# A recurrent attention with a gated feed-forward layer: the ordering list is searched anew with the weight additions one by one, and the last bank goes in two halves

## The chip, the cores and the metric

The kernel runs on one core of one Trainium2 chip. The metric is the device time of one execution in microseconds (us); lower is better. Five engines work side by side: TensorE (PE, with its weight load PEld), VectorE (DVE), ScalarE (ACT), GpSimd (POOL) and SyncE (SP), which issues most of the DMAs.

## The reference

The first part is a recurrence over 768 tokens for 4 batches and 8 heads of 48 dimensions, the second a feed-forward layer on the 3072 tokens:

```python
for t in range(S):
    cur = np.einsum('bhd,bhe->bhde', u[None] * kt, vt)
    y[:, :, t] = np.einsum('bhd,bhde->bhe', rt, state + cur)
    state = w[None, :, :, None] * state + np.einsum('bhd,bhe->bhde', kt, vt)
...
h = x @ w_in                       # 3072 x 384 by 384 x 2048
g = h * np.clip(h + 3.0, 0.0, 6.0) / 6.0
return g @ w_out                   # 3072 x 2048 by 2048 x 384
```

## The kernel before

**Attention.** The recurrence is done in 24 half steps i = 0 to 23 of 64 tokens for two batches (`attention`). `prepare` scales k and r by powers of w (tiles ks and RP), makes the bonus term (rt, bt, X); a *visit* is one block of small TensorE products: `keep` adds k v to the state in the bank U, `scores` of the next step fills the bank SC, `outputs` makes the result from the state St and from X. `choose` puts the masked scores into X (the row named COPY_PREDICATED or "mask"). After a visit VectorE makes the state product St (L710) from U, and ScalarE copies St back into U (L702); the next visit reads both. Visits and state products are numbered from zero by i. From step 6 on a visit holds the scores of the next step too.

**Feed-forward.** The weights come as 64-bit words (raw) and are turned into a high and a low part, w (`weights`: z, cv on VectorE and ScalarE, "CAST w" and "w<-z,w"). Tokens go in 6 groups of 512. In the groups 0 and 1 a unit is one of 16 blocks f of 128 hidden rows: nine products of 512 columns into h (L361), relu and gate (t on ScalarE and VectorE, g on ScalarE and VectorE), nine products into the banks o (L368). The groups 2 to 5 go in two passes of two groups with a scheme that saves products: inputs, weights and intermediate banks are added and subtracted, so that fewer products (`product`, L890) are needed. The sums of the weights for two blocks f and f+1 are made by `sums` into the tile zf: one large addition of w's high and low part (L861) and four small ones on quarters of zf (L864); ScalarE or VectorE rounds zf to S, and VectorE or GpSimd takes the rest (L852). There are 8 such pairs in each of two passes. `second` makes the output products of the one group in the banks o, `beside` those of the other group in the banks h0 (hA), SC (hC) and Y (hD), one bank after the other; VectorE adds a bank divided by 6 to the tile part (L929), and `store` writes it.

**What sets the order.** Every piece is recorded as an operation with its cost on each engine that may do it (`S.add`). `Schedule.order` then makes one list for all engines at build time: among the operations that can start, the one with the highest priority goes first. The priority is the length of what follows plus a number from the table SHIFT; the table HOME fixes the engine of single operations. Operations with `port=True` exclude each other on VectorE and GpSimd in this plan. Where TensorE would be idle, the plan may put dummy products (`warm`, L1071). Only the order of the instructions on each engine goes to the chip; there semaphores set the times.

The additions of `sums` were one operation, on GpSimd alone:

```python
S.add({"pool": 3.0}, ws, ["zf"], emit, 0.0, True, deps=[fresh])
```

The last bank of the program is that of `outside(2, ...)`: `beside` puts two times three products into Y, VectorE adds, SP stores 128 rows of 512 columns.

Of the kernel before, what the change touches and what calls it, by code (L numbers as in the profile page):

```python
# [17 lines left out]
ALU = mybir.AluOpType  # L18
# [188 lines left out]
    "pool", 1191: "dve", 1193: "dve", 1205: "pool", 1209: "act", 1216: "act", 1220: "act", 1258: "dve", 1287: "dve",  # L207
    1289: "dve", 1292: "act", 1294: "pool", 1310: "dve", 1321: "dve", 1333: "dve", 1337: "dve", 1349: "dve", 1376:
    "dve", 1388: "dve", 1399: "dve", 1413: "dve", 1416: "dve", 1450: "pool", 1452: "dve", 1454: "dve", 1489: "dve",
    1493: "act", 1494: "pool", 1516: "dve", 1530: "dve"  # L210
}


# [1020 lines left out]
```

## Time and profile before

| | |
|---|---|
| median of three runs | 479.52 us (478.64 to 482.89) |
| the profiled execution: its time | 478.21 us |
| the profiled execution: its span | 476.1 us |
| TensorE busy | 458.7 us, 96% of the span |
| VectorE busy | 363.1 us, 76% |
| ScalarE busy | 220.3 us, 46% |
| GpSimd busy | 155.6 us, 33% |

The span is what the trace covers; 2.1 us of the execution's time lie around it. Busy shares are means over stages that are unlike each other: the attention steps lie in the first 345 us, the products of the last 120 us stand alone. A product of TensorE overlaps the next, so that its own duration is longer than its pace.

### The profile page before, as it was taken

To read this page: it belongs to the slowest core of one execution; us is meant where nothing else is said; L and a number is where in the kernel's file an instruction comes from. 1 tells how busy PE (TensorE), PEld (TensorE's weight loads), DVE (VectorE), ACT (ScalarE), POOL (GpSimd) and SP (SyncE) were. 2 spreads that over 40 slices of the span, in tenths; PEclk is the share of its full clock that TensorE was granted. 3 is DMA by queue.
4 is the path that set the end of the run, shared out by engine and by line. 5 is a ranking of instruction groups with operands and counts; after the bars stand their busy time and mean duration, and the time that the engine had idled before them with its cause. 6 is when DMAs were issued, how large, how long until landed. Compare 5 with 4: busy or idle time off the path is not lost.

```text
span 476.1 us, 11775 instructions
## 1 busy us (share of the span) xinstructions
PE 458.7 (96%) x4914; PEld 377.6 (79%) x4914; DVE 363.1 (76%) x553; ACT 220.3 (46%) x386; POOL 155.6 (33%) x156
## 2 busy tenths in 40 slices
PE   8889899999998999999999999999999999999994
PEld 6778788888887888777778878888688888888883
DVE  6989999989999983999597686464976456664553
ACT  5465757653434533554443344354653434343441
POOL 2173111124366630364452345235133213321100
PEclk9989999999999999999999999999999999999998
DMA  7977654483434612341220220000120000000003
GB/s 213 271 234 217 215 156 132 141 246 123 125 118 151 194 45 78 91 136 43 77 89 22 79 90 20 8 1 7 47 88 3 1 1 0 1 0 0 1 0 138
DMA packets 27038, 42.91 MB, mean 90 GB/s; under 512 B 4034, under 2 KB 12867, under 8 KB 26979
## 3 DMA queue, kind: packets, MB, share of 16 engines
q1 hardware_dynamic: 26882, 42.00, 29.0%
q8 instruction: 40, 0.66, 0.6%
q14 instruction: 20, 0.16, 0.1%
q10 hardware_dynamic: 96, 0.10, 0.1%
HBM read 35.98 MB, written 4.72 MB: 85 GB/s over the span
## 4 chain that ended last, share of the span: by engine, by line
PE 73%; DVE 16%; issue 3%; DMA 3%; ACT 2%; SPq 1%; ACTq 0%; DVEq 0%
PE o L368 21%; PE h L890 17%; PE h L361 10%; PE Y L368 5%; PE SC L890 4%; PE h L368 4%; PE SC L368 4%; PE Y L890 2%; PE SC L561 2%; DVE ks L458 2%; DMA rT<-rT 2%; PE h L561 1%; PE Y L561 1%; DVE RP L458 1%; DVE g L458 1%
## 5 line engine op out<-in xcount | busy, mean ns | idle before, releaser
L368 PE MATMUL o<-g,w 128*128 128x512 f32 (+1 forms) x594 | 143.0, 385 | 0.7 <-issue 0.7
L368 PEld LDWEIGHTS o<-g,w 128*128 128x128 f32 x594 | 108.8, 188 | 23.1 <-issue 0.9
L361 PE MATMUL h<-XR,w 128*128 128x512 f32 (+1 forms) x306 | 72.2, 380 | 0.2 <-DVE w L458 0.2
L361 PEld LDWEIGHTS h<-XR,w 128*128 128x128 f32 x306 | 54.7, 188 | 11.0 <-DVE w L458 0.5
L890 PE MATMUL h<-XR,w 128*128 128x512 f32 x240 | 62.7, 391 | 0.3 <-DVE Y L1020 0.3
L907 ACT CAST g<-t 128x512 fp32r<-128x512 f32 x64 | 39.3, 621 | 49.2 <-PE Y L368 25.1
L861 POOL TENSOR_TENSOR zf<-w 128x512 f32<-128x512 f32 x16 | 25.9, 1620 | 87.2 <-DVE S L852 87.1
L890 PEld LDWEIGHTS h<-XR,w 128*128 128x128 f32 x240 | 44.7, 188 | 10.4 <-DVE Y L1020 0.7
L852 DVE TENSOR_TENSOR g<-t,g 128x512 fp32r<-128x512 f32 x56 | 42.8, 777 | 9.3 <-ACT g L907 9.2
L901 ACT ACTIVATE t<-h,b 128x512 f32<-128x512 f32 x32 | 22.0, 689 | 54.9 <-PE h L890 42.7
L890 PE MATMUL h<-XR,S 128*128 128x512 f32 x144 | 41.4, 393 | 1.7 <-DVE XR L852 1.1
L864 POOL TENSOR_TENSOR zf<-zf 128x128 f32<-128x128 f32 x64 | 35.0, 548 | 5.0
L766 ACT CAST g<-t 128x512 fp32r<-128x512 f32 (+1 forms) x34 | 20.1, 595 | 34.8 <-DVE t L762 34.8
L890 PEld LDWEIGHTS h<-XR,S 128*128 128x128 f32 x144 | 26.7, 188 | 9.0 <-DVE XR L852 2.0
L760 ACT ACTIVATE t<-h,b 128x512 f32<-128x512 f32 (+1 forms) x34 | 22.5, 662 | 20.4 <-PE h L361 16.4
L1016 DVE TENSOR_TENSOR SC<-h,RP 128x512 f32<-128x512 f32 x16 | 11.2, 698 | 26.0 <-PE h L890 17.6
L762 DVE SCALAR_TENSOR_TENSOR t<-t,h 128x512 f32<-128x512 f32 (+1 forms) x34 | 21.9, 648 | 10.4 <-ACT t L760 10.4
L458 POOL TENSOR_TENSOR w<-z,w 128x768 fp32r<-128x768 f32 x6 | 13.0, 2175 | 48.6 <-DVE w L495 42.9
L458 POOL TENSOR_TENSOR RP<-rT,E 112x512 f32<-112x512 f32 x11 | 17.7, 1609 | 31.7 <-PE Y L561 12.0
L458 DVE TENSOR_TENSOR g<-t,g 128x512 fp32r<-128x512 f32 (+1 forms) x34 | 26.1, 773 | 2.5 <-ACT g L766 2.2
L902 DVE SCALAR_TENSOR_TENSOR t<-t,h 128x512 f32<-128x512 f32 x32 | 21.8, 682 | 6.5 <-ACT t L901 6.4
L561 PE MATMUL SC<-RP,ks 48*64 48x64 f32 (+1 forms) x672 | 25.1, 223 | 0.7 <-DVE ks L458 0.7
(153 smaller groups left out, 855.9 us busy)
## 6 DMA issues: line engine op xcount, KB each, us to landing
raw<-wcat SPq DMA_DIRECT2D x48, 256.0 KB, 3.9
kT<-kT SPq DMA_DIRECT2D x24, 224.0 KB, 4.2
rT<-rT SPq DMA_DIRECT2D x24, 224.0 KB, 4.1
V<-vt SPq DMA_DIRECT2D x24, 192.0 KB, 3.7
kt<-kt SPq DMA_DIRECT2D x22, 192.0 KB, 4.0
rt<-rt SPq DMA_DIRECT2D x16, 192.0 KB, 3.4
outT<-xf SPq DMA_DIRECT2D x9, 256.0 KB, 2.1
outT<-part SPq DMA_DIRECT2D x9, 256.0 KB, 2.0
```

What stands on the lines that cost most here:

```text
L361: nc.tensor.matmul(h, (w_hi, w_lo)[wl][:, f, 0, 128 * j:128 * j + 128], x(j, hl), start=(m == 0 and j == 0), stop=(m == 2 and j == 2))
L368: nc.tensor.matmul(o[m], (w_hi, w_lo)[wl][:, f, 1, 128 * m:128 * m + 128], g(hl), start=(clear and k == 0), stop=(last and k == 2), skip_g ...
L458: emit = lambda e: eng[e].tensor_tensor(out=out, in0=in0, in1=in1, op=op)
L561: nc.tensor.matmul(out, lhsT, rhs, start=start, stop=True, skip_group_check=True)
L760: S.add({"act": 0.13 + 0.23 * ns}, [("h", n % 2), "b3"], [kt_], lambda e: act.activation(out=t[:, :T], in_=h[:, :T], func=AF.Relu, bias=b3 ...
L762: last = S.add({"dve": 0.05 + 0.28 * ns}, [("h", n % 2), kt_], [kt_], lambda e: dve.scalar_tensor_tensor(out=t[:, :T], in0=t[:, :T], scala ...
L852: S.add(costs, reads, writes, lambda e: eng[e].tensor_tensor(out=out(), in0=in0(), in1=in1(), op=op), 0.0, True)
L861: v.tensor_tensor(out=zf, in0=wi[0], in1=wi[1], op=ALU.add)
L864: v.tensor_tensor(out=zf[:, to[0], to[1]], in0=zf[:, a[0], a[1]], in1=zf[:, b[0], b[1]], op=op)
L890: nc.tensor.matmul(bank, stat(f, a)[0](wl), xb(b)[:, hl], start=start and n == 0 and m == 0, stop=True, skip_group_check=True)
L901: S.add({"act": 0.59}, [key, "b3"], [kt_], lambda e: act.activation(out=t, in_=bank, func=AF.Relu, bias=b3, scale=1.0))
L907: S.add({"act": 0.52}, [kt_], [kg + (0,)], lambda e: act.copy(out=gq(r)[:, 0], in_=t))
```

## The change

`sums` is cut into five operations that may each go to GpSimd or VectorE. The planner's costs get two new numbers: a visit of the later steps is 0.15 us longer, and the wait between two operations of TensorE is 0. SHIFT and HOME are searched anew for the resulting list. In the last step of the program the bank of `outside(2)` is made in two halves of 256 columns, the first in Y, the second in the bank o0, each with its own addition and its own store.

```diff
 SHIFT = {
...
-    16: 8.8, 17: 2.6, 18: -0.6, 20: -0.6, 21: -9.9, 22: -1.4, 23: 3.9, 25: -0.6, 26: -0.6, 27: 12.3, 28: -2.2, 29:
...
 HOME = {
-    19: "act", 20: "dve", 21: "dve", 39: "dve", 57: "pool", 75: "dve", 98: "act", 102: "act", 107: "act", 111:
+    19: "pool", 20: "dve", 38: "pool", 39: "dve", 40: "pool", 57: "pool", 58: "pool", 65: "pool", 75: "dve", 76:
...
-                    at[j][x] = max(at[j][x], ready_at + (WAIT["sp"] if "sp" in ops[i][0] else WAIT[e] if x != e else 0.03)
+                    at[j][x] = max(at[j][x], ready_at + (WAIT["sp"] if "sp" in ops[i][0] else WAIT[e] if x != e else 0.0 if e == "pe" else 0.03)
...
-        visit([keep(i)] + ([scores(i + 1)] if joint else []), [outputs(i)], 0.15 if 4 <= i + 1 < EARLY else -0.05)
+        visit([keep(i)] + ([scores(i + 1)] if joint else []), [outputs(i)], 0.15 if 4 <= i + 1 < EARLY else 0.1 if i >= EARLY else -0.05)
...
     def sums(f):
 
-        def emit(e):
-            zf, v = late["zf"], eng[e]
+        zf = lambda a, k: late["zf"][:, a, k]
+        ws = [(k, f + i) for k in ("wh", "wl") for i in range(2)]
+
+        def whole(e):
             wi = [w[:, hl, f:f + 2, 0, 0:256].rearrange("p a (k n) -> p a k n", k=2).bitcast(F32) for hl in range(2)]
-            v.tensor_tensor(out=zf, in0=wi[0], in1=wi[1], op=ALU.add)
-            for to, a, b, op in (((1, 1), (1, 0), (1, 1), ALU.add), ((1, 0), (0, 0), (1, 0), ALU.subtract),
-                                 ((0, 0), (1, 1), (0, 0), ALU.subtract), ((0, 1), (0, 1), (0, 0), ALU.subtract)):
-                v.tensor_tensor(out=zf[:, to[0], to[1]], in0=zf[:, a[0], a[1]], in1=zf[:, b[0], b[1]], op=op)
-        ws = [(k, f + i) for k in ("wh", "wl") for i in range(2)]
-        S.add({"pool": 3.0}, ws, ["zf"], emit, 0.0, True, deps=[fresh])
+            eng[e].tensor_tensor(out=late["zf"], in0=wi[0], in1=wi[1], op=ALU.add)
+        S.add({"pool": 1.5, "dve": 0.6}, ws, ["zf"], whole, 0.0, True, deps=[fresh])
+        for to, a, b, op in (((1, 1), (1, 0), (1, 1), ALU.add), ((1, 0), (0, 0), (1, 0), ALU.subtract),
+                             ((0, 0), (1, 1), (0, 0), ALU.subtract), ((0, 1), (0, 1), (0, 0), ALU.subtract)):
+            S.add({"pool": 0.53, "dve": 0.2}, ["zf"], ["zf"], lambda e, to=to, a=a, b=b, op=op: eng[e].tensor_tensor(
+                out=zf(*to), in0=zf(*a), in1=zf(*b), op=op), 0.0, True)
...
-    def beside(f, m):
-        bank, kb = ((hA, kA), (hC, kC), (hD, kD))[m]
+    def beside(f, m, cols=slice(0, 512), bank=None, kb=None):
+        if bank is None:
+            bank, kb = ((hA, kA), (hC, kC), (hD, kD))[m]
+        n = (cols.stop - cols.start) / 512
+        key = ("part", m) if n == 1 else ("part", m, cols.start // 256)
...
-            S.add({"dve": 0.61}, [kb], [("part", m)], lambda e: dve.scalar_tensor_tensor(
-                out=part[:, m], in0=bank, scalar=1.0 / 6.0, in1=part[:, m], op0=ALU.mult, op1=ALU.add))
+            S.add({"dve": 0.05 + 0.56 * n}, [kb, ("part", m)], [key], lambda e: dve.scalar_tensor_tensor(
+                out=part[:, m, cols], in0=bank, scalar=1.0 / 6.0, in1=part[:, m, cols], op0=ALU.mult, op1=ALU.add))
...
-            def outside(m, f=f - 2 if q else NF - 2, g=ga + 1 if q else ga - 1):
+            def outside(m, f=f - 2 if q else NF - 2, g=ga + 1 if q else ga - 1, halves=False):
+                if halves:
+                    for c, (bank, kb) in enumerate(((hD, kD), (ops[0], "o0"))):
+                        beside(f, m, slice(256 * c, 256 * c + 256), bank[:, :256], kb)
+                        store(g, m, lambda c=c: part[:, m, 256 * c:256 * c + 256], ("part", m, c), 256 * c, 256)
+                    return
...
-                    outside(m, f, ga + 1)
+                    outside(m, f, ga + 1, m == 2)
```

In the built program 13 of the 16 large additions and 40 of the 64 small ones stand on VectorE and the others on GpSimd. The dummy products are 6 of 132 columns and 5 of 156 instead of one of 444, two of 308 and one of 216. From the fourth pair of blocks on, TensorE's order of products is the same but for single visits. The changed lines of `sums` and `beside` are L873, L877 and L944 in the new file, and a line behind the tables has moved by ten to twenty (L368 to L378, L561 to L571, L710 to L720).

VectorE around state product 10 (St0_91 <- U). Before, from the gate of a unit to the second ks behind St:

```order
L458 TENSOR_TENSOR rt1_80<-rt1_80,ubt_94 128x384
L762 SCALAR_TENSOR_TENSOR t0_101<-t0_101,h0_65 128x512
L852 TENSOR_TENSOR S_1664<-zf_1669,S_1664 128x512
L643 TENSOR_TENSOR X0_85<-bt0_89,idc_98 128x512
L458 TENSOR_TENSOR g0_103<-t0_101,g0_103 128x512
L458 TENSOR_TENSOR KH0_107<-kt0_81,TW_93 128x384
L710 TENSOR_TENSOR St0_91<-U_123,E_99 112x384
L681 COPY_PREDICATED X1_86<-mask_106,SC_121 128x512
L458 TENSOR_TENSOR ks1_110<-kT1_78,E_99 112x512
L458 TENSOR_TENSOR ks0_109<-kT0_77,E_99 112x512
```

and now, at the same state product:

```order
L772 SCALAR_TENSOR_TENSOR t0_101<-t0_101,h0_65 128x512
L873 TENSOR_TENSOR zf_1679<-w_61 128x512
L468 TENSOR_TENSOR g0_103<-t0_101,g0_103 128x512
L877 TENSOR_TENSOR zf_1679<-zf_1679 128x128 x4
L772 SCALAR_TENSOR_TENSOR t1_102<-t1_102,h1_66 128x512
L468 TENSOR_TENSOR KH0_107<-kt0_81,TW_93 128x384
L653 TENSOR_TENSOR X0_85<-bt0_89,idc_98 128x512
L691 COPY_PREDICATED X1_86<-mask_106,SC_121 128x512
L720 TENSOR_TENSOR St0_91<-U_123,E_99 112x384
L810 TENSOR_SCALAR xf_1678<-o1_68 128x512
```

The mask of X1, which reads the scores of visit 10, stood behind St and now stands directly ahead of it; the two ks behind St are no longer there, and five additions of a weight sum stand ahead of it on VectorE.

TensorE between visits 9 and 10. The rows with U, Y and SC are a visit's; before:

```order
L561 MATMUL Y_122<-X1_86,V1_84 48x64 x2
L561 MATMUL SC_121<-RP0_87,ks0_109 64x64 x2
L561 MATMUL Y_122<-X1_86,V1_84 48x64 x2
L368 MATMUL o0_67<-g0_103,w_61 128x512 x3
L368 MATMUL o1_68<-g0_103,w_61 128x512 x3
L368 MATMUL o2_69<-g0_103,w_61 128x512 x3
L361 MATMUL h0_65<-XR_100,w_61 128x512 x9
L561 MATMUL U_123<-V0_83,KH0_107 48x48 x2
```

and now:

```order
L571 MATMUL Y_122<-X1_86,V1_84 48x64 x2
L571 MATMUL SC_121<-RP0_87,ks0_109 64x64 x2
L571 MATMUL Y_122<-X1_86,V1_84 48x64 x2
L378 MATMUL o0_67<-g0_103,w_61 128x512 x3
L378 MATMUL o1_68<-g0_103,w_61 128x512 x3
L378 MATMUL o2_69<-g0_103,w_61 128x512 x3
L371 MATMUL h0_65<-XR_100,w_61 128x512 x9
L378 MATMUL o0_67<-g1_104,w_61 128x512 x3
L378 MATMUL o1_68<-g1_104,w_61 128x512 x3
L378 MATMUL o2_69<-g1_104,w_61 128x512 x3
L371 MATMUL h1_66<-XR_100,w_61 128x512 x9
L571 MATMUL U_123<-V0_83,KH0_107 48x48 x2
```

A block of nine products into o and one of nine into h1 have come in between. Between visits 10 and 11 there were three such blocks (o, h1, o) and there are two now (o, h0).

TensorE's last products, of the bank Y and what follows it. Before:

```order
L368 MATMUL h0_65<-g1_104,w_61 128x512 x3
L368 MATMUL h0_65<-g3_1667,w_61 128x512 x3
L368 MATMUL SC_121<-g1_104,w_61 128x512 x3
L368 MATMUL SC_121<-g3_1667,w_61 128x512 x3
L368 MATMUL Y_122<-g1_104,w_61 128x512 x3
L368 MATMUL Y_122<-g3_1667,w_61 128x512 x3
```

and now:

```order
L378 MATMUL h0_65<-g1_104,w_61 128x512 x3
L378 MATMUL h0_65<-g3_1677,w_61 128x512 x3
L378 MATMUL SC_121<-g1_104,w_61 128x512 x3
L378 MATMUL SC_121<-g3_1677,w_61 128x512 x3
L378 MATMUL Y_122<-g1_104,w_61 128x256 x3
L378 MATMUL Y_122<-g3_1677,w_61 128x256 x3
L378 MATMUL o0_67<-g1_104,w_61 128x256 x3
L378 MATMUL o0_67<-g3_1677,w_61 128x256 x3
```

The last six products of 512 columns have become six of 256 into Y and six of 256 into o0. VectorE's addition and SP's store, one of 512 columns before, follow each half with 256 columns.

## Rows read from the trace of the kernel before

**Rows 1.** The page's busy times, share of the span and instructions of each engine

```profile
PE 458.7 (96%) x4914; PEld 377.6 (79%) x4914; DVE 363.1 (76%) x553; ACT 220.3 (46%) x386; POOL 155.6 (33%) x156
```

**Rows 2.** Busy us in stretches: stretch, length, PE PEld DVE ACT POOL, PEclk, DMA, GB/s

```profile
20.00:60.00 40.00, 36.21 (x975) 32.28 (x971) 38.08 (x58) 24.72 (x39) 16.33 (x10) 0.96 0.72 223
140.00:160.00 20.00, 18.38 (x369) 15.16 (x360) 20.00 (x29) 8.12 (x17) 12.71 (x11) 1.00 0.46 144
200.00:300.00 100.00, 98.97 (x1142) 79.92 (x1141) 79.58 (x124) 43.38 (x79) 48.54 (x50) 1.00 0.23 67
345.00:465.00 120.00, 120.00 (x531) 99.07 (x530) 71.54 (x111) 49.87 (x81) 26.63 (x33) 1.00 0.03 9
```

**Rows 3.** TensorE's waits, waiting group and releaser: us in all, times, longest

```profile
PE Y L561 <- issue: 1.4, 1, 1.4
...
PE h L890 <- DVE XR L852: 1.1, 2, 0.7
PE U L561 <- ACT U L702: 0.9, 1, 0.9
...
PE SC L561 <- DVE ks L458: 0.7, 1, 0.7
...
PE h L890 <- ACT XR L828: 0.6, 1, 0.6
```

**Rows 4.** Timeline 145 to 151 us: start, length, engine, row [idle before and releaser]

```profile
144.82 1.73 POOL L861 TENSOR_TENSOR zf<-w 128x512 f32<-128x512 f32 x1
145.33 1.65 DVE L458 TENSOR_TENSOR KH<-kt,TW 128x384 f32<-128x384 f32 x1
...
146.90 0.55 DVE L710 TENSOR_TENSOR St<-U,E 112x384 f32<-112x384 f32 x1
...
147.36 0.71 DVE L681 COPY_PREDICATED X<-mask,SC 128x512 f32<-128x512 uint8 x1
147.53 0.48 ACT L702 COPY U<-St 112x384 f32<-112x384 f32 x1 [3.56 <-DVE St L710]
...
148.07 0.25 PE L561 MATMUL U<-V,KH 64*48 64x48 f32 x2 [0.89 <-ACT U L702]
```

**Rows 5.** Groups of GpSimd: count, busy us, mean ns of one, idle before

```profile
L864 POOL TENSOR_TENSOR zf<-zf 128x128 f32<-128x128 f32 x64 | 35.0, 548 | 5.0
L861 POOL TENSOR_TENSOR zf<-w 128x512 f32<-128x512 f32 x16 | 25.9, 1620 | 87.2 <-DVE S L852 87.1
```

**Rows 6.** Groups of VectorE by shape, same columns

```profile
L490 DVE SCALAR_TENSOR_TENSOR cv<-raw,cv 128x768 int32<-128x768 int32 x16 | 17.0, 1071 | 0.6 <-ACT cv L489 0.6
L458 DVE TENSOR_TENSOR KH<-kt,TW 128x384 f32<-128x384 f32 x15 | 13.5, 903 | 0.0
...
L852 DVE TENSOR_TENSOR xf<-xf 128x512 f32<-128x512 f32 x7 | 4.8, 683 | 0.1
L495 DVE CAST w<-z 128x768 fp32r<-128x768 f32 x8 | 4.4, 555 | 0.1
...
L762 DVE SCALAR_TENSOR_TENSOR t<-t,h 128x256 f32<-128x256 f32 x4 | 1.5, 416 | 0.0
...
L540 DVE TENSOR_TENSOR E<-E 112x128 f32<-112x128 f32 x1 | 0.3, 292 | 0.0
```

**Rows 7.** Timeline from 468 us to the end

```profile
470.00 0.69 DVE L929 SCALAR_TENSOR_TENSOR part<-Y,part 128x512 f32<-128x512 f32 x1 [0.67 <-PE Y L368]
```

**Rows 8.** DMAs: issues of the page, then a queue and an issue from 470.5 to 476.2

```profile
outT<-part SPq DMA_DIRECT2D x9, 256.0 KB, 2.0
...
q8 instruction: 1, 0.02, 1.8%
...
outT<-part SPq DMA_DIRECT2D x1, 256.0 KB, 3.9
```

**Rows 9.** Chain of work that ended last, 43 to 56 us: start, us, what

```profile
43.77 1.08 PE h L361 x9
...
53.76 2.07 PE h L361 x9
```

More of the change, by code (lines that the diff above doesn't have):

```diff
@@ L63 @@
 SHIFT = {
[125 rows of a table removed]
[128 rows of a table added]
 }
 HOME = {
-    19: "act", 20: "dve", 21: "dve", 39: "dve", 57: "pool", 75: "dve", 98: "act", 102: "act", 107: "act", 111:
-    "act", 120: "act", 121: "dve", 130: "dve", 135: "dve", 137: "pool", 141: "pool", 155: "act", 159: "act", 160:
-    "dve", 166: "pool", 171: "dve", 174: "pool", 196: "act", 201: "dve", 216: "pool", 226: "dve", 231: "dve", 241:
-    "act", 246: "dve", 251: "pool", 253: "dve", 254: "pool", 255: "dve", 275: "dve", 276: "pool", 286: "dve", 287:
-    "dve", 289: "pool", 344: "dve", 345: "pool", 362: "dve", 363: "pool", 373: "act", 378: "pool", 393: "pool", 441:
@@ L196 @@
-    "dve", 443: "dve", 472: "dve", 475: "dve", 479: "pool", 514: "pool", 516: "dve", 517: "dve", 518: "pool", 519:
-    "dve", 521: "pool", 540: "dve", 541: "pool", 542: "pool", 543: "dve", 563: "dve", 580: "dve", 583: "dve", 587:
-    "pool", 604: "dve", 607: "pool", 608: "pool", 609: "pool", 611: "pool", 640: "dve", 644: "dve", 645: "dve", 647:
-    "dve", 664: "pool", 668: "dve", 669: "dve", 703: "dve", 705: "pool", 711: "dve", 719: "dve", 720: "pool", 722:
-    "dve", 743: "pool", 754: "dve", 763: "dve", 765: "pool", 766: "pool", 780: "pool", 805: "dve", 814: "dve", 816:
@@ L201 @@
-    "pool", 817: "dve", 818: "dve", 819: "dve", 821: "dve", 835: "act", 843: "dve", 845: "dve", 846: "dve", 857:
-    "dve", 877: "dve", 880: "dve", 898: "dve", 902: "dve", 903: "pool", 914: "dve", 925: "dve", 934: "pool", 937:
-    "dve", 938: "pool", 939: "dve", 941: "pool", 961: "pool", 963: "pool", 965: "dve", 966: "dve", 988: "dve", 1001:
-    "pool", 1002: "dve", 1004: "dve", 1018: "pool", 1020: "dve", 1022: "act", 1023: "dve", 1054: "dve", 1056: "dve",
-    1057: "dve", 1058: "dve", 1061: "dve", 1081: "dve", 1085: "act", 1117: "pool", 1118: "pool", 1122: "pool", 1139:
@@ L206 @@
-    "act", 1140: "dve", 1151: "dve", 1175: "dve", 1179: "pool", 1182: "dve", 1184: "dve", 1187: "pool", 1189:
[L207 to L210, printed above, removed]
+    19: "pool", 20: "dve", 38: "pool", 39: "dve", 40: "pool", 57: "pool", 58: "pool", 65: "pool", 75: "dve", 76:
@@ new lines @@
+    "pool", 89: "sp", 92: "sp", 93: "sp", 94: "sp", 98: "act", 102: "dve", 107: "act", 116: "act", 125: "dve", 130:
+    "dve", 136: "dve", 137: "dve", 141: "dve", 155: "act", 159: "act", 160: "dve", 165: "pool", 166: "pool", 171:
+    "dve", 174: "pool", 196: "act", 211: "dve", 215: "act", 216: "pool", 231: "pool", 241: "dve", 245: "act", 246:
+    "dve", 254: "dve", 271: "dve", 275: "dve", 276: "dve", 282: "dve", 284: "dve", 287: "dve", 289: "dve", 314:
+    "act", 330: "dve", 340: "dve", 345: "pool", 362: "dve", 363: "pool", 378: "pool", 388: "act", 392: "act", 393:
@@ new lines @@
+    "pool", 443: "dve", 472: "dve", 474: "dve", 475: "dve", 479: "pool", 517: "dve", 518: "pool", 519: "pool", 521:
+    "pool", 540: "pool", 541: "pool", 542: "pool", 543: "dve", 563: "dve", 565: "dve", 582: "dve", 583: "dve", 587:
+    "pool", 604: "dve", 606: "dve", 607: "dve", 608: "pool", 609: "pool", 611: "pool", 645: "dve", 647: "dve", 664:
+    "pool", 666: "pool", 667: "pool", 669: "dve", 671: "pool", 707: "dve", 708: "dve", 710: "dve", 711: "dve", 713:
+    "pool", 715: "pool", 719: "dve", 720: "pool", 722: "dve", 724: "dve", 725: "dve", 727: "pool", 758: "pool", 767:
@@ new lines @@
+    "dve", 769: "dve", 770: "pool", 772: "dve", 788: "dve", 791: "pool", 813: "dve", 822: "dve", 826: "dve", 827:
+    "dve", 829: "pool", 847: "act", 849: "dve", 851: "dve", 852: "dve", 854: "dve", 855: "dve", 856: "dve", 857:
+    "act", 858: "pool", 880: "dve", 891: "dve", 893: "dve", 894: "pool", 896: "pool", 910: "dve", 915: "pool", 916:
+    "pool", 918: "dve", 919: "pool", 930: "dve", 952: "dve", 953: "dve", 955: "pool", 957: "dve", 977: "pool", 979:
+    "pool", 980: "dve", 981: "pool", 983: "dve", 984: "dve", 985: "dve", 986: "dve", 1017: "dve", 1021: "pool",
@@ new lines @@
+    1022: "dve", 1024: "dve", 1040: "dve", 1041: "dve", 1042: "pool", 1043: "dve", 1069: "dve", 1078: "dve", 1081:
+    "pool", 1083: "dve", 1085: "dve", 1105: "dve", 1109: "pool", 1111: "dve", 1145: "dve", 1147: "pool", 1148:
+    "dve", 1150: "pool", 1166: "dve", 1169: "dve", 1170: "pool", 1172: "dve", 1183: "pool", 1194: "dve", 1211:
+    "dve", 1213: "dve", 1214: "dve", 1216: "dve", 1217: "pool", 1219: "pool", 1221: "dve", 1225: "dve", 1226: "dve",
+    1239: "pool", 1240: "dve", 1242: "dve", 1243: "dve", 1245: "act", 1252: "act", 1254: "dve", 1256: "act", 1263:
@@ new lines @@
+    "dve", 1289: "dve", 1291: "dve", 1292: "dve", 1295: "dve", 1296: "dve", 1297: "dve", 1298: "dve", 1320: "dve",
+    1327: "act", 1332: "dve", 1336: "dve", 1337: "pool", 1338: "dve", 1339: "dve", 1340: "dve", 1343: "dve", 1354:
+    "dve", 1365: "dve", 1377: "dve", 1381: "pool", 1382: "dve", 1383: "dve", 1384: "dve", 1385: "dve", 1408: "dve",
+    1424: "pool", 1425: "dve", 1427: "dve", 1428: "dve", 1440: "dve", 1467: "dve", 1468: "pool", 1469: "dve", 1470:
+    "pool", 1472: "dve", 1483: "dve", 1506: "pool", 1508: "dve", 1512: "pool", 1514: "dve", 1549: "pool", 1551:
@@ L211 @@
+    "pool", 1552: "pool", 1553: "dve", 1554: "dve", 1556: "dve", 1557: "act", 1558: "pool", 1569: "dve", 1594: "dve"
 }
@@ L916, in second @@
               [f"o{m}" for m in ms] + ["ffn"], emit, count=6 * len(ms))
-    def beside(f, m):
-        bank, kb = ((hA, kA), (hC, kC), (hD, kD))[m]
+    def beside(f, m, cols=slice(0, 512), bank=None, kb=None):
[3 more added lines that the diff above has]
+        key = ("part", m) if n == 1 else ("part", m, cols.start // 256)
         def emit(e):
             for i in range(2):
-                project(nc, {m: bank}, w_hi, w_lo, f + i, lambda hl: gq(2 * i + 1)[:, hl], i == 0, i == 1, [m])
-        S.add({"pe": 1.364}, [("g", r, hl) for r in (1, 3) for hl in range(2)] + [(k, f + i) for k in ("wh", "wl") for i in range(2)],
+                project(nc, {m: bank}, w_hi, w_lo, f + i, lambda hl: gq(2 * i + 1)[:, hl, cols], i == 0, i == 1, [m])
+        S.add({"pe": 0.08 * (n < 1) + 1.364 * n}, [("g", r, hl) for r in (1, 3) for hl in range(2)] + [(k, f + i) for k in ("wh", "wl") for i in range(2)],
               [kb, "ffn"], emit, count=12)
```

252 rows, old and new, of the table SHIFT are left out of this document.

## The prediction

> **What bounds the kernel now.** I read the busy times first. TensorE is busy 458.7 of the 476.1 us span, VectorE 363.1, GpSimd 155.6 [rows 1]. By stretches, TensorE is full in 345 to 465 us and nearly full in 200 to 300, where VectorE is busy 79.58 of 100 us; in 20 to 60 VectorE is busy 38.08 of 40 us, and in 140 to 160 it is busy all 20 while TensorE has only 18.38 [rows 2]. So TensorE's work is the bound, and a change that leaves its products alone can win only TensorE's idle time and the tail behind its last product. The list of TensorE's waits shows how little that is: 0.9 us for a ScalarE copy into U, 0.7 us for ks, 1.1 and 0.6 us for XR, besides gaps that the profile charges to no wait, the longest 1.4 us [rows 3]. The remaining rows of that list are such gaps, or 0.6 us or less, or stand before 20 us.
>
> One of these waits can be followed backwards [rows 4]. GpSimd starts the first addition of a weight sum at 144.82 us and holds it 1.73 us. VectorE's KH product starts at 145.33 and takes 1.65 us; the state product St, of nearly its size (112x384), takes 0.55. St, queued behind KH, starts at 146.90; the copy into U at 147.53; TensorE's visit, which reads U, at 148.07, after 0.89 us idle. The ks product behind St then makes the same visit wait 0.7 us in its second half.
>
> **The change, part by part.**
>
> *The sums one by one.* Before, each of 8 pairs of weight blocks in two passes makes one GpSimd job: one addition of 1620 ns and four of 548 ns, 16 jobs, 25.9 + 35.0 = 60.9 us [rows 5]. Now 13 of the 16 large and 40 of the 64 small ones stand on VectorE. A two-input product of 128x512 takes VectorE 683 ns, one of 112x128 takes 292 [rows 6]: 13 x 0.683 + 40 x 0.292 = 8.9 + 11.7 = 20.6 us more on VectorE, and 13 x 1.62 + 40 x 0.548 = 43.0 us less on GpSimd. What hides the 20.6 us is TensorE. Counted by the order (state products and visits from zero), two large and six small additions (3.1 us) come between state products 8 and 10, none up to 16, four large and eleven small (5.9 us) from there to 21, the last, mostly in what is now 200 to 300 us, with 20 us of VectorE idle, and 7 large and 23 small (11.5 us) after it, where VectorE has 48 of 120 us free in 345 to 465 alone [rows 2]. I cost them at nothing. Without that cover the 3.1 us would stand on the path.
>
> The Trainium skill, "SBUF — State Buffer", section "Who interferes with whom", says that a VectorE instruction with two SBUF inputs and a GpSimd instruction that reads SBUF take one port as an exclusive lock for the whole instruction. The KH row agrees: it ends 0.43 us after the GpSimd addition does. The mean KH product of 903 ns against the 0.55 of St says the same of fifteen of them [rows 6].
>
> *The visits at 148 us.* The searched list changes what leads to this wait. The waiting visit is number 11. VectorE now has the mask of X and then state product 10 directly behind visit 10, the GpSimd sum at that place is gone, and TensorE has four blocks of nine products instead of two between visits 9 and 10, and two instead of three from there to 11. A block of nine is 2.07 us [rows 9], so from visit 9 to state product 10 VectorE has 4.1 us more time, and by its order about 1 us more work: its backlog should be gone when visit 10 ends. From there the mask (0.71), St (0.55) and the copy (0.48) [rows 4] need 1.7 us, and the two blocks give 4.1. Both waits should go: -0.9 - 0.7 = -1.6 us. Bounds: 0, if another product becomes the late one, and -1.6.
>
> *The splits of XR and the other gaps after 190 us.* They come from the same cause, a VectorE or ScalarE piece that stands behind a longer one; 1.1 + 0.6 us [rows 3]. A new search with longer visits removes some and makes some. I take half: -0.8 us; bounds 0 and -1.7.
>
> *The first 60 us.* VectorE is the one that is full here. Up to state product 2 the new list has two RP and two KH products fewer (to GpSimd): 2 x 0.68 + 2 x 0.55 = 2.5 us less. Up to number 6 it has five rows more, all of weights: one cv (1071 ns), one z, taken like a cast, and three casts (555 each, from ScalarE), against two 512-column products fewer: 1.07 + 4 x 0.555 - 1.37 = +1.9 us [rows 6]. The weights of the first unit are ready sooner, since the cast moves from ScalarE to VectorE directly behind its operand, and visits 5 and 6 have more in front. Gain and loss meet where TensorE becomes full at about 50 us: I take 0, bounds -1.4 and +1.9. Eleven dummy products of 132 and 156 columns instead of four of 216 to 444 (1572 against 1276 columns) stand where TensorE waits for St and cost nothing; the waits charged to issue stay.
>
> *The tail.* Six products of 512 columns become two sets of six of 256. Nine of 256 take 1.08 us and nine of 512 take 2.07 [rows 9], so 12 x 0.120 - 6 x 0.230 = +0.06 us. The last VectorE addition, 0.69 us [rows 7], becomes 416 ns [rows 6]: -0.27. The last store lands 3.9 us after its issue, though the median of its kind is 2.0; a code load of one packet goes through the same engines then [rows 8]. It has half the bytes now: between 0 and -0.6 us, I take -0.3. Sum -0.5; bounds -0.2 and -0.8. The first half's addition and store hide behind the second half's six products (0.72 us).
>
> The Trainium skill, "DMA: Bandwidth & Descriptors", section "Anatomy of one DMA — SWDGE (gpsimd) path", gives a fixed cost of about 2 us plus the bytes by 436 GB/s, measured for another way of issuing. By that estimate 128 KB less are 0.3 us; no run here has shown a 128 KB store.
>
> *The planner's constants* (the visit's extra 0.1, the same-engine wait of 0.0) reach the chip only through the order.
>
> **Sum.** -0.5 - 1.6 - 0.8 + 0 = -2.9 us on the profiled execution's 478.21, which is 475.3. That execution lies 0.4 us under the lowest and 1.3 under the median of the three runs shown; I add 0.4: 475.7.
>
> **Rivals.** (1) The gaps move instead of going: every search leaves about as many small waits, and only the tail is won. For it speaks that the waits after 190 us have releasers on VectorE and on ScalarE; against it, that the largest one has a cause that is removed. 478.2 - 0.5 = 477.7, with run offset 478.1. (2) The lock costs more than the waits show. With 43 us of GpSimd time gone, VectorE's stretched products (KH alone 15 x 0.35 = 5.3 us) shrink in the stages where VectorE is full, so the early chain wins its 1.4 us too and all 1.7 us after 190 go: 478.2 - 0.8 - 1.6 - 1.7 - 1.4 = 472.7, with offset 473.1. Against it: in most of these stages TensorE was full anyhow. (3) The early stage loses its 1.9 us and the rest holds: 475.3 + 1.9 = 477.2, with offset 477.6. (4) Slower: VectorE falls behind in the stage that was already at 20 of 20 us. The 3.1 us of sums there plus one more two-block gap missed by 0.9 us stand on the path, the tail is won: 478.2 + 3.1 + 0.9 - 0.5 = 481.7, with offset 482.1. It decides if state product 10 starts later than two blocks of nine products, 4.1 us, after visit 10. Against it: the four-block gap. (5) Nothing changes at all: the tail's halves cannot do less than the 0.2 us, so this is inside (1).
>
> **Chances.** Forecast 0.42 (its own range 474 to 477), (1) 0.18, (2) 0.22, (3) 0.10, (4) 0.08. One per cent, about what a measurement of this kernel can tell from no change, is 4.8 us on the median 479.5: faster means under 474.7, slower over 484.3. Rival (2) is faster, and a quarter of the forecast's own range (0.11) is: 0.33. Of (4) about half, with more than one sum late, is slower: 0.04. The rest is 0.63. The range runs from 472.3, a little under (2), to 479.6, over (1) and (3) by the run offset of the median; outside it are (4) and the lower end of (2).
>
> **What would show it.** Visit 11 starts without idle time, and the KH and g products before it last 0.55 and 0.68 us; TensorE's waits after 190 us sum to under 1.7 us; state product 6 starts within 1.5 us of where it did; VectorE is busier by 14 to 21 us in all and GpSimd less by about 43; from TensorE's last product to the end of the span there are about 5.6 us instead of 6.1. Wrong would be an idle TensorE before a visit behind a VectorE row of the sums, or a first block of nine 512-column products that starts over 2 us later.

## The result, and the profile after

| | before | after |
|---|---|---|
| median | 478.53 us (477.25 to 482.89, 20 runs) | 484.44 us (480.31 to 488.42, 20 runs) |
| ratio after to before, 95% interval | | 1.0105 (1.008 to 1.013) |
| the profiled execution, and its span | 478.21, 476.1 us | 488.42, 486.6 us |

The change made the kernel 1% slower, some 5 to 6 us, where 475.7 us and a gain were forecast. The profiled execution of after is the slowest of its twenty, so its losses are larger than those of a usual one; sizes below come from medians wherever a run has them, places come from the trace.

The page's busy times of after, which answer to [rows 1], and its TensorE clock in 40 slices (a 9 is 90% of full speed or more):

```profile
PE 464.8 (96%) x4934; PEld 385.7 (79%) x4934; DVE 375.4 (77%) x609; ACT 217.0 (45%) x381; POOL 114.8 (24%) x106
PEclk9979889999999999999999999999989999999998
```

and the clock row of before:

```profile
PEclk9989999999999999999999999999999999999998
```

GpSimd lost 40.8 us, near the 43 that were worked out; VectorE gained 12.3, a little under the 14 to 21 that were named. TensorE's busy time grew by 6 us although its products are the same and its dummy products add little: the clock rows show why. Before, the clock is lowered in the third slice alone; now it is lower still there, and lowered in the fifth and sixth slice and once more at about 355 us. Which half of the program lost is seen in stretches. First the row of 0 to 75 us for the kernel before (columns as in [rows 2]):

```profile
0.00:75.00 75.00, 68.17 (x1405) 58.12 (x1406) 68.36 (x116) 43.44 (x80) 21.84 (x25) 0.98 0.73 218
```

then after, with the stretches of [rows 2]:

```profile
0.00:75.00 75.00, 63.13 (x1373) 55.39 (x1374) 61.41 (x105) 34.70 (x67) 21.61 (x27) 0.91 0.68 192
20.00:60.00 40.00, 30.83 (x820) 28.93 (x816) 35.95 (x56) 17.38 (x29) 11.25 (x7) 0.87 0.69 193
140.00:160.00 20.00, 20.00 (x327) 16.35 (x325) 19.73 (x34) 7.80 (x16) 9.17 (x9) 1.00 0.35 107
200.00:300.00 100.00, 98.56 (x1024) 80.39 (x1023) 85.32 (x141) 45.83 (x84) 30.08 (x27) 1.00 0.24 74
345.00:465.00 120.00, 117.81 (x512) 96.56 (x511) 76.70 (x129) 49.07 (x82) 18.04 (x18) 0.99 0.04 14
```

In the first 75 us TensorE is busy 5.0 us less than before, and its granted clock is 0.91 instead of 0.98 (the same 75 us with about 5 us less of full clock). From 140 to 160 it is busy all 20 us instead of 18.38, and from 75 to 190, where the later start of the same work matters little, 114.94 of 115 instead of 113.38: the gain that was forecast there came. From 345 it has an idle place that before did not have. TensorE's waits of after name the places (us in all, times, longest), to be read against [rows 3]:

```profile
PE U L571 <- ACT g L776: 3.5, 1, 3.5
PE h L902 <- ACT xf L809: 2.2, 1, 2.2
PE SC L571 <- issue: 2.0, 2, 1.2
PE h L1091 <- issue: 1.7, 1, 1.7
...
PE h L902 <- DVE XR L862: 1.4, 1, 1.4
PE h L371 <- DVE w L505: 1.1, 1, 1.1
```

The 0.9 us for the copy into U and the 0.7 us for ks, on which the forecast rested, are gone. New are 3.5 us before visit 6, 1.1 us for the first weights, 1.7 us inside the dummy products, and behind 190 us one wait of 1.4 and one of 2.2 us. TensorE and VectorE around visit 6, from the timeline of after:

```profile
51.73 0.55 DVE L720 TENSOR_TENSOR St<-U,E 112x384 f32<-112x384 f32 x1
52.20 0.68 DVE L653 TENSOR_TENSOR X<-SC,idc 128x512 f32<-128x512 f32 x1
52.79 0.68 DVE L468 TENSOR_TENSOR RP<-rT,E 112x512 f32<-112x512 f32 x1
53.39 0.72 DVE L691 COPY_PREDICATED X<-mask,SC 128x512 f32<-128x512 uint8 x1
54.00 0.68 DVE L468 TENSOR_TENSOR X<-ks,RP 112x512 f32<-112x512 f32 x1
54.59 0.42 DVE L772 SCALAR_TENSOR_TENSOR t<-t,h 128x256 f32<-128x256 f32 x1
54.93 0.56 DVE L468 TENSOR_TENSOR KH<-kt,TW 128x384 f32<-128x384 f32 x1
...
55.58 0.25 PE L571 MATMUL U<-V,KH 64*48 64x48 f32 x2 [3.52 <-ACT g L776]
```

State product 5 starts at 51.73 us, where before it started at 43.14, and KH ends at 55.49, 0.09 us ahead of the visit. The row names a ScalarE gate, but of the rows shown VectorE's KH is the last one that the visit reads: in this trace VectorE is the late engine. Behind the 3.5 us of idle TensorE its clock is at half, as the row of that stretch says (0.50 behind the GpSimd column):

```profile
56.60:63.40 6.80, 6.80 (x107) 6.01 (x98) 6.20 (x10) 4.12 (x6) 2.63 (x1) 0.50 0.58 167
```

### The profile page after: what moved, and what is told of

It is laid out like the page before. It is cut to its first block, busy times and chain, and to the rows that moved or that the text cites. A ratio compares the mean times of both kernels' runs of the same rounds, so it can differ in the third digit from the quotient of the medians.

```text
span 486.6 us, 11802 instructions
## 1 busy us (share of the span) xinstructions
PE 464.8 (96%) x4934; PEld 385.7 (79%) x4934; DVE 375.4 (77%) x609; ACT 217.0 (45%) x381; POOL 114.8 (24%) x106
## 4 chain that ended last, share of the span: by engine, by line
PE 80%; DVE 10%; DMA 2%; issue 2%; ACT 2%; SPq 1%; POOL 0%; DVEq 0%; ACTq 0%
PE o L378 23%; PE h L902 17%; PE h L371 11%; PE SC L902 4%; PE h L378 4%; PE SC L378 4%; PE Y L378 4%; PE SC L571 3%; PE Y L571 2%; PE Y L902 2%; PE U L571 2%; PE h L571 2%; DVE XR L862 1%; DVE xf L862 1%; PE o L571 1%
## 5 line engine op out<-in xcount | busy, mean ns | idle before, releaser
L378 PE MATMUL o<-g,w 128*128 128x512 f32 (+1 forms) x600 | 144.3, 385 | 0.0
L378 PEld LDWEIGHTS o<-g,w 128*128 128x128 f32 x600 | 109.2, 188 | 22.3
L371 PE MATMUL h<-XR,w 128*128 128x512 f32 (+1 forms) x306 | 73.4, 385 | 1.5 <-DVE w L505 1.1
L371 PEld LDWEIGHTS h<-XR,w 128*128 128x128 f32 x306 | 56.2, 192 | 12.6 <-DVE w L505 1.2
L902 PEld LDWEIGHTS h<-XR,w 128*128 128x128 f32 x240 | 45.7, 191 | 10.1 <-DVE Y L1035 0.4
L862 DVE TENSOR_TENSOR g<-t,g 128x512 fp32r<-128x512 f32 x54 | 37.4, 708 | 4.5 <-ACT g L919 4.4
L877 POOL TENSOR_TENSOR zf<-zf 128x128 f32<-128x128 f32 x24 | 13.0, 541 | 96.2 <-DVE zf L873 59.4
L571 PEld LDWEIGHTS U<-V,KH 64*48 64x48 f32 x704 | 18.8, 127 | 10.4 <-issue 6.1
L571 PE MATMUL SC<-RP,ks 48*64 48x64 f32 (+1 forms) x672 | 25.8, 226 | 1.2 <-issue 0.7
L571 PE MATMUL U<-V,KH 64*48 64x48 f32 x704 | 21.3, 213 | 4.0 <-ACT g L776 3.5
L468 DVE TENSOR_TENSOR g<-t,g 128x512 fp32r<-128x512 f32 (+1 forms) x34 | 23.3, 685 | 1.6 <-ACT g L776 1.4
```

The costliest lines, as they stand in the source:

```text
L371: nc.tensor.matmul(h, (w_hi, w_lo)[wl][:, f, 0, 128 * j:128 * j + 128], x(j, hl), start=(m == 0 and j == 0), stop=(m == 2 and j == 2))
L378: nc.tensor.matmul(o[m], (w_hi, w_lo)[wl][:, f, 1, 128 * m:128 * m + 128], g(hl), start=(clear and k == 0), stop=(last and k == 2), skip_g ...
L468: emit = lambda e: eng[e].tensor_tensor(out=out, in0=in0, in1=in1, op=op)
L571: nc.tensor.matmul(out, lhsT, rhs, start=start, stop=True, skip_group_check=True)
L862: S.add(costs, reads, writes, lambda e: eng[e].tensor_tensor(out=out(), in0=in0(), in1=in1(), op=op), 0.0, True)
L902: nc.tensor.matmul(bank, stat(f, a)[0](wl), xb(b)[:, hl], start=start and n == 0 and m == 0, stop=True, skip_group_check=True)
```

## The experiments

Each run has its own runs of the kernel before beside it on the same chip; ratios are to those.

**Which part of the program.** The kernel was cut in its emission order: what the plan starts before 100 us is taken from the one list, what comes later from the other.

```diff
+    first = [
...
+    ]
+    for e, i in first:
+        if i < 0:
+            warm(-i, float(e))
+        else:
+            S.ops[i][2](e)
+    told = {i for _, i in first if i >= 0}
...
     for start, _, e, i in done:
+        if i in told:
+            continue
```

Old start, new rest:

> The changed kernel with the former order, engines and dummy products for everything planned before 100 us; from there the new order. Theory A (the new order of the first 70 us is what costs: there the trace of after falls 11 us behind that of before in TensorE's finished products, and later it gains 0.7 us net): the loss is gone and the later gain stays, 475.3 to 477.8 us, the first visit that waits over 3 us is gone, and TensorE's clock is at half in one stretch of the first 70 us instead of three. Theory B (the later part costs: sums on VectorE, the new order after 100 us): 483 to 485 us, as after.

Measured: 479.22 us, ratio 0.9995 (0.9969 to 1.002). New start, old rest:

> The kernel before with the new order, engines and dummy products for everything planned before 100 us, and the former order behind it; no other part of the change is in it. Theory A (the new order of the first 70 us costs): 484 to 489 us, as slow as after or slower, since the later gains are not in it. Theory B (the later part costs): 478.5 us, as before.

Measured: 485.31 us, ratio 1.0122 (1.0094 to 1.015). Both speak for theory A and against B: the start alone makes the kernel slow, by 5.3 us with the later part new and 5.8 with it old (differences of the ratios, times 479 us). But the old start gave no gain over the kernel before; the forecast's later gain was missing too, and that is taken up below.

**Dummy products and sums.**

```diff
     done, fill = S.order()
+    fill = []
```

> The changed kernel without its eleven dummy products of the first 36 us; they compute nothing that is used. Theory C (the many small dummy products stand ahead of visits that could already start, since TensorE was late there, and cost up to 3.8 us): 480 to 481.5 us, visit 4 starts at about 32.5 us instead of 35.1. Theory A, with waits on VectorE as the cause: 484 us or more, since what follows waits for weights that VectorE finishes at 41 us, and TensorE, idle for longer, would have its clock at half in more stretches.

Measured: 485.89 us, ratio 1.014 (1.011 to 1.0171). Theory C falls. Its row of 0 to 75 us shows the other side:

```profile
0.00:75.00 75.00, 62.59 (x1350) 54.83 (x1351) 61.24 (x105) 34.74 (x67) 22.26 (x27) 0.84 0.68 193
```

TensorE is busy about as little as in after, and its clock is 0.84: the dummy products are no load on the path that this run shows, and without them the clock is lower. The time itself is 1.5 us over that of after, which the two intervals do not separate.

```diff
-        S.ops[i][2](e)
+        S.ops[i][2]("pool" if S.ops[i][0].get("pool") in (1.5, 0.53) else e)
```

> The changed kernel with all 80 additions of the weight sums on GpSimd, each at its place in the new order. Theory A (the start costs): 484 us, and up to 6 us more, since GpSimd takes 43 us more and holds VectorE's two-input products again. Theory B (the 20.6 us of sums on VectorE cost): 478 to 480 us.

Measured: 483.55 us, ratio 1.0117 (1.0078 to 1.0155), no different from after. The 53 additions cost nothing on VectorE that this run can tell (its interval is 1.8 us to either side), and nothing is won by them either.

**The later gain that was missing.** The run with the old start has the same new wait as after, 2.2 us behind xf. From the timeline of after (L862 on GpSimd is the second half of a gate, g <- t, g):

```profile
346.61 2.56 DVE L862 TENSOR_TENSOR XR<-xf,XR 128x512 fp32r<-128x512 f32 x2
...
346.88 3.43 POOL L862 TENSOR_TENSOR g<-t,g 128x512 fp32r<-128x512 f32 x2
...
349.09 1.77 DVE L862 TENSOR_TENSOR xf<-xf 128x512 f32<-128x512 f32 x1
350.78 0.68 DVE L862 TENSOR_TENSOR XR<-xf,XR 128x512 fp32r<-128x512 f32 x1
...
351.38 0.69 DVE L1031 TENSOR_TENSOR SC<-h,RP 128x512 f32<-128x512 f32 x1
...
352.21 0.94 PE L902 MATMUL h<-XR,S 128*128 128x512 f32 x3 [2.19 <-ACT xf L809]
```

While GpSimd makes two gate pieces, VectorE's two XR take 2.56 us and its xf 1.77; behind them stands the product of SC, which must read h before TensorE may write it. (The row names ScalarE's xf; that one ends within 0.02 us of this product and stands behind the same xf of VectorE.) In the plan these gate pieces came behind that xf and XR, since it keeps two such operations off the port at once; on the chip GpSimd began as soon as its data were there.

```diff
-        S.ops[i][2](e)
+        S.ops[i][2]("dve" if i in (1237, 1239) else e)
```

> The run with the old start, with two gate pieces that the new order gives to GpSimd (the two g <- t, g that took 3.43 us at 338 us there) on VectorE, behind the product of SC from h and RP. Theory D (GpSimd's two pieces run while VectorE makes XR and xf, stretch these by 2.3 us, and so make the 2.2 us wait of TensorE at 343 us, behind which its clock falls for 3.4 us, up to 1.7 us more): the XR and xf take 0.69 us each, the wait is gone, and the median is 2.2 to 3.9 us under the 479.2 of the old start alone, 475.3 to 477.0. Rival E (VectorE is the late one there, lock or no lock, since it now has two rows more): the wait stays at 1 us or more or moves behind the next product, and the median is within 1 us of 479.2.

Measured: 476.43 us, ratio 0.9938 (0.9915 to 0.9962), 2.8 us under the old start alone. Its timeline at the same place:

```profile
338.03 1.46 DVE L862 TENSOR_TENSOR XR<-xf,XR 128x512 fp32r<-128x512 f32 x2
...
339.42 0.68 DVE L862 TENSOR_TENSOR xf<-xf 128x512 f32<-128x512 f32 x1
340.02 0.68 DVE L862 TENSOR_TENSOR XR<-xf,XR 128x512 fp32r<-128x512 f32 x1
340.62 0.68 DVE L1031 TENSOR_TENSOR SC<-h,RP 128x512 f32<-128x512 f32 x1
341.23 0.68 DVE L862 TENSOR_TENSOR g<-t,g 128x512 fp32r<-128x512 f32 x1
341.45 0.93 PE L902 MATMUL h<-XR,S 128*128 128x512 f32 x3
```

No idle time stands at TensorE's row any more, and the clock stays up: a stretch behind this product, first of the run with the old start, then of this run (the number behind the GpSimd column is the clock):

```profile
344.50:347.90 3.40, 3.40 (x10) 2.63 (x9) 3.37 (x7) 1.21 (x2) 0.47 (x1) 0.50 0.32 119
```

```profile
341.50:345.00 3.50, 3.50 (x16) 2.90 (x17) 3.50 (x7) 0.75 (x2) 0.00 (x0) 1.00 0.24 89
```

So theory D holds, with its second half: the wait of 2.2 us costs more than itself, since 3.4 us at half clock follow. With the new start the same edit gave:

> The changed kernel with the new start, and the two gate pieces of 346 us on VectorE. Theory D (GpSimd's two pieces make the wait of 2.2 us at 352 us and the fall of the clock behind it): 2 to 3.5 us under the 484.4 of after, 481 to 482.5, since the old start alone gave 479.2 and, with the pieces moved, 476.4. If the two places work together, it stays near 484. It is the base of the three next runs.

Measured: 481.94 us, ratio 1.0055 (1.0032 to 1.0079), 2.5 us under after: the edit is worth about the same with either start. So the loss at this place does not hang on that of the start. The other late wait, 1.4 us for XR, was tried in the same way:

```diff
-        S.ops[i][2]("dve" if i in (1237, 1239) else e)
+        S.ops[i][2]("dve" if i in (720, 770, 1237, 1239) else e)
```

> The run with the old start and the two gate pieces on VectorE (476.4 us), with two more GpSimd rows on VectorE, at their places of the plan: the xf that GpSimd begins at 194.69 us there, 1.65 us before its planned turn, and the RP behind it. Theory D, for a second place (a GpSimd row that starts when its data are there, not when the plan has VectorE's rows done, stretches VectorE's xf and XR from 0.69 to 1.78 and 1.67 us and makes TensorE's wait of 1.43 us at 198.4): both rows take 0.69 us, the wait is gone, and the time is 1.0 to 1.5 us lower, about 475.2. Rival E (VectorE itself is late there): the wait stays over 0.7 us, and the time within 0.5 us of 476.4.

Measured: 474.96 us, ratio 0.9913 (0.9889 to 0.9938). The timeline of the run without this edit, then with it:

```profile
194.69 1.53 POOL L862 TENSOR_TENSOR xf<-xf 128x512 f32<-128x512 f32 x1 [16.62 <-DVE xf L862]
194.99 1.78 DVE L862 TENSOR_TENSOR xf<-xf 128x512 f32<-128x512 f32 x1
...
196.69 1.67 DVE L862 TENSOR_TENSOR XR<-xf,XR 128x512 fp32r<-128x512 f32 x1
...
198.42 0.50 PE L902 MATMUL h<-XR,S 128*128 128x512 f32 x1 [1.43 <-DVE XR L862]
```

```profile
194.07 0.69 DVE L862 TENSOR_TENSOR xf<-xf 128x512 f32<-128x512 f32 x1
...
195.45 0.84 PE L902 MATMUL h<-XR,S 128*128 128x512 f32 x3
195.74 0.69 DVE L862 TENSOR_TENSOR XR<-xf,XR 128x512 fp32r<-128x512 f32 x1
```

This version, the changed kernel with the old start and four GpSimd rows on VectorE, beats both kernels: 4.8 us under the 479.79 us of before beside it.

The Trainium skill, "SBUF — State Buffer", section "Who interferes with whom", calls the port of VectorE and GpSimd an exclusive lock that the first comer holds for a whole instruction. These rows agree: VectorE's xf and XR go from 1.67 to 1.78 us back to 0.68 and 0.69 once GpSimd's rows (two in 3.43 us, and an xf of 1.53 with an RP of 1.64 behind it) are gone.

**The tail.**

```diff
-                    outside(m, f, ga + 1, m == 2)
+                    outside(m, f, ga + 1)
```

> The kernel with the old start and the two gate pieces on VectorE, and with the last bank in one piece of 512 columns with one store, as before. Theory F (the end of the program does not wait for the last store but for the jump of SyncE behind its last issue, 2.8 us, and the second half's issue delays that jump by 0.3 to 0.5 us): the time is that of the run with halves within 0.3 us, and 6.0 to 6.2 us lie between TensorE's last product and the end, in both. The prediction's tail step: 0.5 us slower than with halves, 6.1 against 5.6 us.

Measured: 476.66 us, ratio 0.9953 (0.9938 to 0.9969), against 476.43 with halves: the halves win nothing that can be measured. The intervals would leave room for 0.5 us; the traces say more. From TensorE's last product to the end are 6.15 us before and 6.25 after, 6.17 and 6.25 in this run and in that with halves (from the ends of the last rows in each trace). SyncE's waits near the end, before and then after:

```profile
SPq L1102 <- SPq L1102: 3.1, 2, 2.9
```

```profile
SPq L1122 <- SPq L1122: 2.8, 1, 2.8
```

L1102 and L1122 are the branch behind the last store and the semaphore instructions that follow it. In before the branch ends 1.2 us after the last product, and SyncE's next instruction comes 2.9 us later, at 4.1. One of the following instructions waits 0.2 us more, the second wait of that row; it is the one for the last store, which lands at about 4.6. In after the branch ends at 1.6, because the second store is issued behind the first, and the next instruction comes at 4.3; no wait for a store is left. So the halves took away 0.2 us and gave it back in the later branch. The Trainium skill, "Runtime: NRT & Kernel Launch", section "Instruction fetch mechanics", says that a taken branch outside the loaded code waits for a load; that fits the 2.8 us, but no run here took the branch away, so that the branch sets the end is read from the traces and not shown by a run.

**What in the start costs.** Two runs cut the start once more, at 36 us of the plan:

> The changed kernel with the former order (and the former three dummy products) for everything planned before 36 us, which is visits 0 to 4 and the first weights, and the new order from there. Theory G (the first 36 us cost: the smaller dummy products, later XR and weights, a longer idle TensorE and a clock that falls there): 479 to 481 us. Theory H (what follows from 36 to 100 us costs: weights, KH and gates on VectorE before visits 5 to 7): 483 to 485 us.

Measured: 483.92 us, ratio 1.0109 (1.0084 to 1.0133).

> The changed kernel with the former order for what is planned from 36 to 100 us, and the new order before and behind it. Theory G (the first 36 us cost): 483 to 485 us. Theory H (36 to 100 us cost): 479 to 481 us. If both this run and its counterpart stay near 482, each part carries about half.

Measured: 483.54 us, ratio 1.0115 (1.0087 to 1.0144). Neither G nor H: each half alone costs as much as both. In the first, TensorE waits 3.3 us before visit 6; in the second, 1.9 us for the first weights; the reading is that where TensorE is late from the one, the other wait hides behind it, and no run shows this by itself. Next, single rows were moved back, on the run with the new start and the gates on VectorE (481.94 us):

```diff
-        S.ops[i][2](e)
+        S.ops[i][2]({1237: 'dve', 1239: 'dve', 102: 'act', 125: 'act', 129: 'act', 120: 'act'}.get(i, e))
```

> The run with the new start and the gates moved, with one z and three casts of weights that the new order gives to VectorE between 34 and 44 us of the plan back on ScalarE, at their places. Theory I (VectorE's rows are the path there): 4 x 0.555 = 2.2 us less than that run, at least 1 us of it seen, and TensorE's wait for w and for visit 6 shrink by it. Rival J (TensorE's own lateness after visit 3 and its clock carry the loss): within 0.7 us of that run.

Measured: 479.84 us, ratio 1.0015 (0.999 to 1.0041): 2.1 us faster (1.9 by the ratios, whose intervals leave some 1.7 us to either side): theory I, with about the size of the four rows.

```diff
-        S.ops[i][2](e)
+        S.ops[i][2]({1237: 'dve', 1239: 'dve', 251: 'pool', 254: 'pool'}.get(i, e))
```

> The run with the new start and the gates moved, with RP and KH of visit 6 back on GpSimd, which has nothing else to do from 45 to 58 us. Theory I: KH is the last thing that visit 6 waits for; without the two rows (0.68 + 0.55 us) on VectorE and with KH ready at about 48 us, the visit starts about 1.2 to 3 us sooner, and the run is 1 to 3 us faster. Rival J: within 0.7 us.

Measured: 482.19 us, ratio 1.0057 (1.0037 to 1.0077). No gain: KH was the last input of visit 6 in the profile, but not what set the time. In the trace of this run the 3.0 us before visit 6 are gone, and between 10 and 60 us the list of TensorE's waits names no other engine; what is left there are gaps that are charged to issue, 7.5 us of them instead of 5.0, mostly these:

```profile
PE SC L571 <- issue: 4.3, 2, 3.2
PE h L1091 <- issue: 2.3, 1, 2.3
```

These are single executions; the medians of the two runs are nearly the same. Both edits together:

> Both edits at once: one z and three casts back on ScalarE, RP and KH of visit 6 back on GpSimd. Theory I: 3 to 4.5 us under the run with the new start and the gates moved, near 478, and VectorE's stretch from state product 4 to 5 is 7.5 to 8 us instead of 9.9. Rival J: within 1 us of that run, about 481.

Measured: 480.75 us, ratio 1.0023 (1.0006 to 1.0039): not better than the weights' rows alone, and VectorE still takes 10.0 us from state product 4 to 5, where theory I had 7.5 to 8. 3.4 us stay between 479.84 and the 476.43 of the old start. Three runs asked for them, each with one queue's rows exchanged:

> The run with the new start, the gates moved and the casts back on ScalarE (479.8 us), with SyncE's loads of the first 60 us of the plan in the former order and all other engines in the new one. 3.4 us are left between it and the same kernel with the old start (476.4). Theory K (the new order of loads: V for visit 3 lands at 23.96 us instead of 22.16, the fourth raw weights are issued at 24.5 instead of 21.0): 476.5 to 478.3 us. Rival L (the dummy products and TensorE's code loads carry the rest) and rival M (the order on VectorE and GpSimd does): 479 to 481 us.

Measured: 486.35 us, ratio 1.0122 (1.0101 to 1.0142).

> The counterpart: the old start with the gates moved (476.4 us), with SyncE's loads of the first 60 us of the plan in the new order. Theory K: 478 to 480 us. Rivals L and M: within 1 us of 476.4, up to 2 more where loads now come in an order that the old rows do not want.

Measured: 480.92 us, ratio 1.0014 (0.9994 to 1.0035).

> The run with the new start, the gates moved and the casts back on ScalarE (479.8 us), with the former dummy products (one of 444 and two of 308 columns) at the places of the six of 132 and the five of 156. Rival L: visit 3 no longer waits for a code load among the dummy products (1.35 us, and five more dummies behind it), 476.5 to 478.3 us. Theory K and rival M: 479 to 481 us.

Measured: 483.95 us, ratio 1.0066 (1.0034 to 1.0098). Each of these three exchanges is slower than the list it was made in, by the ratios 5.1, 3.6 and 2.4 us of 479, and slower than any of the theories said. The loads of neither start fit the rows of the other, and the old dummy products do not fit the new rows. That the new loads cost the old start 3.6 us shows how much hangs on their order, but theory K falls, since the old loads do not help the new rows. Which piece of the new start holds the last 3.4 us stays open.

The traces show one thing that these runs did not single out. Of TensorE's gaps between 10 and 60 us that are charged to issue, 56 of the 60 of 0.4 us or more, in all eighteen traces, end 1.2 to 1.6 us after a 16 KB load on the instruction queue (q8 in the DMA records) ends. So the gaps go with loads of code. With the gates moved they sum to 2.2 to 4.5 us in the three traces with the old start and its loads, and to 5.0 to 7.5 in the four with the new start, its loads and its dummy products. The difference is about the size of what is left. But a trace is one execution, the run with SyncE's old loads has only 1.2 us of such gaps and is among the slowest, and no run moved the loads of code alone: that they hold the last 3.4 us is not shown.

## Why the prediction was wrong, by its own steps

**The first 60 us: this step failed.** It was costed at 0 with bounds -1.4 and +1.9. The runs give 5.3 us with the later part new and 5.8 with it old. What was counted was right as far as it went: four rows of weights on VectorE, costed at 4 x 0.555 = 2.2 us, are worth about 2. But it was a count of one engine's rows in the stage that runs without slack, taken for a bound on the time. The order of SyncE's loads and the fit of the lists to each other were not costed at all. Neither was the clock, which fell at 55 us behind an idle TensorE. And the waits charged to issue, which were to stay, sum to 4.8 us between 10 and 60 us instead of 3.5. In the profiled pair the idle time of TensorE and the lost clock are about 5 us each; over the twenty runs of after, the time falls with the mean clock (correlation -0.70, 3.5 us for each 0.01 of clock). How much of the 5.3 us is clock was not isolated. The sign by which this step could be known is plain: state product 6 starts at 59.47 us instead of 51.55, where 1.5 us were allowed.

**The gaps after 190 us: failed too.** Forecast -0.8, bounds 0 and -1.7, no loss. The waits of the former list there did go, but two new ones came, 1.4 and 2.2 us, the second with a fallen clock behind it. Taking them away brought 1.2 and 2.7 us by the ratios. The cause is the one that the prediction read at 148 us, a GpSimd row ahead of VectorE's; it was read as a thing the change removes, and not looked for in the new order, which has it at two other places.

**The visits at 148 us: right.** -1.6 us forecast; TensorE is busy 1.6 us more both in the 20 us there and from 75 to 190 us, and no wait of TensorE is left between 60 and 190 us, so visit 11 starts without idle time.

**The sums: near in price, right in cover.** They take 749 and 329 ns instead of 683 and 292:

```profile
L877 DVE TENSOR_TENSOR zf<-zf 128x128 f32<-128x128 f32 x40 | 13.2, 329 | 0.7
...
L873 DVE TENSOR_TENSOR zf<-w 128x512 f32<-128x512 f32 x13 | 9.7, 749 | 0.1
```

That is 22.9 us instead of 20.6, and with all of them on GpSimd the time is the same within 1.8 us. Rival (2), that 43 us less of GpSimd would win by itself, falls with it.

**The tail: failed.** Forecast were -0.5 us; the traces have 6.25 us behind the last product instead of 6.15. VectorE's last addition did take 0.42 us, and the last stores landed 3.0 us from issue (median of the two halves) instead of 3.9. But the end waited for the store for 0.2 us only; ahead of that stood SyncE's branch, which the second issue delays.

**The rivals.** Rival (3) named the right stage, with 1.9 us where 5 to 6 were lost; the engine that it named carries about 2 of them. Rival (4) looked for the slower case at 140 to 160 us, where the change gained.

**The sum again**, from ratios against 479 us: the later part gives -1.6 (148 us) + 2.7 (the wait at 352 us) + 1.2 (the wait at 207 us) and, so that the old start's -0.2 comes out, -2.5 for the former waits that are gone, which no run measured by itself (in the trace of before the waits after 190 us sum to 2.8 us, more than the 1.7 that the prediction counted); the start gives +5.3. That is +5.1 us, the ratio of 1.0105.

## What to carry to other kernels

When a hand-made or searched order changes a stage in which every engine is near its limit, don't cost the stage by the rows that one engine gains or loses: follow its first waits through all queues, the loads too, and count on the loss side that TensorE's clock may fall behind an idle place, as it did here behind 2.2 and 3.5 us, though not behind the 1.4 us at 207 us. A plan that keeps GpSimd and VectorE apart on paper holds nothing back on the chip: look in the new order for every GpSimd row whose data are ready before its turn and that stands beside a late two-input row of VectorE; moving four such rows to VectorE won 3.9 us here, by the ratios. A shorter last store is worth something only if nothing else ends with it.

## What the runs showed of the hardware that was not expected

- Between SyncE's branch behind the last store and its next instruction pass 2.7 to 3.1 us, in the traces of before, after and the two runs compared for the tail.
- Idle places of TensorE of 2.2 us (352 us) and 3.5 us (55 us) were each followed by a stretch at half clock, 3.4 and 6.8 us long; without the wait at 352 us the stretch was not there.
- Without the eleven dummy products of the start the time was 1.5 us longer, which the intervals do not separate, and TensorE's mean clock 0.972 to 0.977 in four executions, with them 0.979 to 0.996 in twenty.
- TensorE lost 1.35 to 2.5 us in the middle of the dummy products at 24 us, charged to issue, in after and in the runs with the new start and the gates moved. These gaps end 1.4 to 1.5 us after a 16 KB load of the instruction queue, as nearly all gaps of this kind here do; no run moved such a load.
